# First chunk's q kept in fp32: its bias from one-column products without weight loads in chunk 1, its phi in chunk 3

## The chip, the cores and the metric

The kernel runs on one core of a Trainium2 chip. The metric is the device time of one execution in microseconds. Five engines work side by side, each on its own list of instructions in order, and they wait for each other by semaphores: PE (TensorE, matrix products, into the eight banks of PSUM; its weight loads are listed as PEld), ACT (ScalarE), DVE (VectorE), POOL (GpSimd) and SP (SyncE, which here only sends DMA transfers, in its own order). In the profile a "q" behind a name (SPq) is that engine's instruction queue.

## What is computed

One block with adaptive layernorm: linear attention, then a gated feed-forward part, on 2048 tokens of width 1024. The change lies in the attention's front: layernorm, scale and shift by columns of c's modulation, and the q and k projections with their phi.

```python
mod = (_silu(c) @ w_mod).reshape(c.shape[0], 6, 1, -1)      # sa, ca, ga, sb, cb, gb
h = _layernorm(x, axis=-1) * (1 + ca) + sa
qkv = (h @ wqkv) ...                                        # 32 heads of 32
phi = lambda t: jnp.where(t > 0, t + 1, jnp.exp(t)) + 1e-06
pq, pk = (phi(q), phi(k))
kv = jnp.einsum('bhsd,bhse->bhde', pk, v)
z = jnp.einsum('bhsd->bhd', pk)
o = jnp.einsum('bhqd,bhde->bhqe', pq, kv) / (jnp.einsum('bhqd,bhd->bhq', pq, z)[..., None] + 1e-06)
x = x + ga * (o @ wo)
...
x = x + gb * (silu(h2 @ w_gate) * (h2 @ w_up) @ w_down)     # h2: layernorm of x, scale cb, shift sb
```

## The kernel before, in words

The 2048 tokens go in four chunks of 512, a chunk in four tiles of 128 tokens (tiles 4 to 7 are chunk 1, 12 to 15 chunk 3). The width 1024 goes in eight slices of 128, called dt. Every operation is recorded in the order of the program text; each engine gets its own in that order, and the waits are worked out from the overlaps of what is read and written in SBUF, and from the PSUM banks (lines 63 to 94 and 130 to 166). A write waits for the last writer and the readers of every byte that it covers.

Chunk 0 is special. Its normalized x is transposed on PE while the first loads still arrive. h0_first and h0_scale_only (520, 540) put x times (1+ca) into HT[:, 0]; HT[:, 1] holds the raw transposed x of dt 4 to 7. q_part (685) adds products to the q groups, one group (nt) of 128 output columns in one PSUM bank, as the weights' slices arrive. The shift sa comes later: mod_sc (504) makes columns of the modulation with one-column products, fin_sa (515) copies them out, bias_mm (528) multiplies them with wq, also in one-column products, each with a weight load of its own, and bias_fin (534) copies the eight sums to BIASQ. For dt 6 and 7 the shift is applied before the product. Then q_phi (789) takes each bank to phi: phi_evac (654) does exp and relu on ACT, and phi_flush (666), two groups at a time, the clamp of the exp and the sum on DVE. For a k group, relu is left out, and DVE reads the bank itself (scalar_tensor_tensor into PKT), so that the bank is free only then. E1 and RL have four slots.

After chunk 0's q come its eight k groups (704), then for chunks 1 to 3 eight k groups and eight q groups each (837). Work of other kinds is hung behind a group by its number, in the tables qside, kside, s1, s2 and s3. Layernorm of later tiles: statistics on DVE (462) or as two passes with sums on ACT (act_stats, 574, whose elementwise output is thrown away, for tiles below 8 into HT[:, 1, 0:2, :]), the power on POOL, the normalization ln1_xn on DVE (479), a transpose by DMA into HT (th_dma, 489), and the scale and shift in place, th_mod (493), on DVE, for chunks 2 and 3 every second slice on ACT. macc (711) adds up a row of the modulation from eight slices of STG on DVE, macc_split and mod_red finish it. next_bank (692) deals out the PSUM banks: in turn over eight, from the 40th group on over five.

Behind chunk 3 comes the G stage (909 on): 16 groups of k-transposed times normalized x, with the denominators (den, 937), the reciprocals sent to HBM and read back (RB), kvt_mm (962) on WV, then the output projection and the feed-forward part, some 630 us. The change doesn't touch these.

SP's loads, in order: x of chunk 0, w_mod's ca and wq in pieces, wsa's second half, wq 6 and 7, wsa's first half, two tiles of x, wk's first half, two more, wk's second half, x of tiles 8 to 11 (410 to 431).

Of the kernel before, what the change touches and what calls it, by code (L numbers as in the profile page):

```python
# [5 lines left out]
FP32 = mybir.dt.float32  # L6
# [256 lines left out]
def bass_adaLN_cond__linear_attn_block__swiglu_ffn__prompt_kernel(  # L263
# [22 lines left out]
    with ExitStack() as es:  # L286
# [52 lines left out]
        HT = T("ht", 120 * KB, [128, 2, NDT, 512], BF16)  # L339
        WO = T("wo", 120 * KB, [128, NHG, D], BF16)  # L340
# [74 lines left out]
        sa_load(1)  # L415
# [3 lines left out]
        for j in range(2):  # L419
            P.dma("x1_%d" % j, XRES[:, 4 + j, :], xv[:, 4 + j, :])  # L420
        for i in (1, 0):
            P.dma("wk0%d" % i, WQK[:, 4 * i:4 * i + 4, 1024:1536], wqkvv[:, 4 * i:4 * i + 4, 1024:1536])
        for j in range(2, 4):
            P.dma("x1_%d" % j, XRES[:, 4 + j, :], xv[:, 4 + j, :])
# [68 lines left out]
        def th_mod(ch, dt):  # L493
            buf = ch % 2
            if dt % 2 == 0 or ch == 1:
                P.dve("tensor_scalar", out=HT[:, buf, dt, :], in0=HT[:, buf, dt, :], scalar1=MODCOL[:, 0, dt:dt + 1],
                      scalar2=MODCOL[:, 1, dt:dt + 1], op0=ALU.mult, op1=ALU.add)
            else:
                P.act("activation", out=HT[:, buf, dt, :], in_=HT[:, buf, dt, :], func=ACT.Identity,
                      scale=MODCOL[:, 0, dt:dt + 1], bias=MODCOL[:, 1, dt:dt + 1])  # L500
# [23 lines left out]
        def h0_shift(dt):  # L524
            P.dve("tensor_scalar", out=HT[:, 0, dt, :], in0=HT[:, 0, dt, :], scalar1=MODCOL[:, 1, dt:dt + 1],
                  scalar2=None, op0=ALU.add)

        def bias_mm(dts):
            for nt in range(NDT):
                for dt in dts:  # L530
                    P.pe("matmul", out=PS[:, 0, 16 + nt:17 + nt], lhsT=WQK[:, dt, nt * 128:(nt + 1) * 128],
                         rhs=MODTMP[:, dt:dt + 1], start=False, stop=(dt == 3), skip_group_check=True)

        def bias_fin():
            P.dve("tensor_copy", out=BIASQ[:], in_=PS[:, 0, 16:24])
# [17 lines left out]

        def h0_scale(dt):
            P.dve("tensor_scalar", out=HT[:, 0, dt, :], in0=HT[:, 1, dt, :], scalar1=MODCOL[:, 0, dt:dt + 1],
                  scalar2=MODCOL[:, 1, dt:dt + 1], op0=ALU.mult, op1=ALU.add)
# [97 lines left out]
        def phi_evac(bank, dst, bias=0.0):  # L654
            i = phi_ctr[0] % 4
            phi_ctr[0] += 1
            P.act("activation", out=E1[:, i, :], in_=PS[:, bank, :], func=ACT.Exp, bias=bias)
            if not isinstance(dst, tuple):
                P.act("activation", out=RL[:, i, :], in_=PS[:, bank, :], func=ACT.Relu, bias=bias)
            phi_pend.append((i, dst, bank))  # L660
            if len(phi_pend) == 2:
                phi_flush()
# [29 lines left out]
        def next_bank():  # L692
            i = qk_ctr[0]
            qk_ctr[0] += 1
            return (1, 2, 3, 4, 6, 7, 5, 0)[i % 8] if i < 40 else i % 5 + 1

        def q_group(ch, nt):
            buf, bank = ch % 2, next_bank()
            for dt in range(NDT):
                P.pe("matmul", out=PS[:, bank, :], lhsT=WQK[:, dt, nt * 128:(nt + 1) * 128],  # L700
                     rhs=HT[:, buf, dt, :], start=(dt == 0), stop=(dt == NDT - 1))
            phi_evac(bank, PQT[:, nt, ch * 512:(ch + 1) * 512])

        def k_group(ch, nt):
            buf, bank = ch % 2, next_bank()
            for i, dt in enumerate((6, 7, 4, 5, 0, 1, 2, 3) if ch == 0 else range(NDT)):
                P.pe("matmul", out=PS[:, bank, :], lhsT=WQK[:, dt, D + nt * 128:D + (nt + 1) * 128],
                     rhs=HT[:, buf, dt, :], start=(i == 0), stop=(i == 7))
# [36 lines left out]
        def q_phase_chunk0(side):  # L745
# [7 lines left out]
            for nt in range(7):  # L753
# [5 lines left out]
                q_part(nt, qb[nt], (2, 3))  # L759
            act_stats(4)  # L760
            for nt in range(7):
                if nt == 4:
                    mod_sc(WSA, 0, range(6, 8))
                    fin_sa(6, 2)
                    for dt in (6, 7):
                        h0_scale(dt)
                q_part(nt, qb[nt], (4, 5))
            mod_sc(WSA, 0, range(4, 6))
            fin_sa(4, 2, True)
            for nt in range(7):  # L770
                if nt == 2:
                    bias_mm((4, 5))
                q_part(nt, qb[nt], (6,))
            for nt in range(7):
                if nt == 1:
                    mod_sc(WSA, 0, range(4))
                    fin_sa(0, 4, True)
                    ln_ops[1][0]()
                    ln_ops[1][1]()
                if nt == 4:  # L780
                    bias_mm(range(4))
                    bias_fin()
                q_part(nt, qb[nt], (7,))
            ln_ops[1][2]()
            ln1_rstd1(5)
# [3 lines left out]
            q_phi = lambda nt: phi_evac(qb[nt] if nt < 7 else 0, PQT[:, nt, 0:512], bias=BIASQ[:, nt:nt + 1])  # L789
            for i, dt in enumerate((4, 5, 0, 1, 2, 3, 6, 7)):  # L790
                P.pe("matmul", out=PS[:, 0, :], lhsT=WQK[:, dt, 896:1024], rhs=HT[:, 0, dt, :], start=(i == 0),
                     stop=(i == 7))
            for dt in (4, 5):
                h0_shift(dt)
            ln1_xn(5)
            th_dma(5)
            for dt in range(4):
                h0_shift(dt)
            ln1_xn(4)
            th_dma(4)  # L800
            for nt in range(8):
                q_phi(nt)
                for f in side.get(nt, []):
                    f()
# [5 lines left out]
        qside, kside = {}, {}  # L810
        ln_ops = [ln1_stats_ops(4 + jj) for jj in range(4)]

        def ln_x1(jj):
            for f in ln_ops[jj]:
                f()
            ln1_rstd1(4 + jj)
        for f in ln_ops[2]:
            add(qside, 1, f)
        for f in ln_ops[3]:
            add(qside, 1, f)  # L820
        add(qside, 1, lambda: ln1_rstd2(6))
        for jj in range(2, 4):
            add(qside, 3, lambda jj=jj: ln1_xn(4 + jj))
            add(qside, 3, lambda jj=jj: th_dma(4 + jj))
        for dt in range(NDT):
            add(kside, 1, lambda dt=dt: th_mod(1, dt))
        for jj, k in ((0, 3), (1, 4)):
            add(kside, k, lambda jj=jj: act_stats(10 + jj))
        q_phase_chunk0(qside)
# [25 lines left out]
        for i in range(NDT):  # L855
            add(s1, 8 + i, lambda i=i: stg_load(i))
            add(s2, 1 + i, lambda i=i: wv_load(i))
# [13 lines left out]

        ln_half(2, s1, 0, 0, 1)
# [11 lines left out]
        for kt in range(NDT):  # L884
            add(s2, 4 + kt, lambda kt=kt: macc(STG, kt))
        add(s2, 13, macc_split)
        add(s2, 13, lambda: P.dma("stg1", STG[:], wmv[:, :, 4096:5120]))
        for kt in range(NDT):
            add(s3, 4 + kt, lambda kt=kt: macc(STG, kt))
        add(s3, 14, macc_split)  # L890
        add(s1, 7, lambda: P.pool("memset", ap=MROW[:], constant=0.0))
        add(s1, 7, lambda: P.pool("memset", ap=ZHL[:], constant=0.0))
        s3.setdefault(2, []).extend([mod_red, mod_row_a])
# [321 lines left out]
```

## Time and profile before

| | us |
|---|---|
| median of 3 runs (827.87 to 829.02) | 828.6 |
| the profiled execution's own span, first to last instruction | 827.0 |
| first product of q | 12.71 |
| chunk 0's q phi on DVE, first to last | 31.60 to 39.9 |
| first product of the G stage | 127.27 |
| DMA at 20 to 30 us | 361 GB/s |

| operation (mean time of one) | ns |
|---|---|
| product 128x512 on PE / its weight load | 379 / 98 |
| one-column product | 163 |
| ACT exp or relu from PSUM, no bias / bias from a tile | 604, 600 / 704, 710 |
| DVE read of a k bank (scalar_tensor_tensor) | 682 |
| DVE clamp / sum of a q group | 283 / 414 |
| DVE macc, 128x1024 fp32 | 1279 |
| DVE bn_stats, 512 wide | 675 |

How to read it: an instruction's time holds its latency too, so that products and small instructions overlap; where a cost matters, the distance from start to start is used. A product's end is modelled. In a line of the order of time, "x55" means that 55 of one form came in a row, and a few per cent of matmul records can be missing. "[1.54 <-DMA ht<-xres]" is idle time before the instruction, and what ended it. The granted PE clock is full all through.

### The profile page before, as it was taken

Reading aid. Unit: us, or ns where it says so; the run is one execution under the profiler, and the core shown is the slowest. Engines: PE = TensorE matmul, PEld = TensorE weight load, DVE = VectorE, ACT = ScalarE, POOL = GpSimd, SP = SyncE. Lnnn points to the kernel's source line nnn. Section 1 sums busy time; section 2 is a strip of 40 time slices with the busy share of each in tenths; the row PEclk is TensorE's granted clock in tenths of the full one; section 3 lists DMA queues with packets and bytes.
Section 4 is the critical chain, followed back from the end, with each engine's and each line's share of the span. In section 5 each row is a group of like instructions: output and inputs, shape, how many; then the busy total and the mean of one; then the engine's idle time right before and its main releaser. Section 6 shows DMA issues by size and latency. Waiting matters only on the chain.

```text
span 827.0 us, 10428 instructions
## 1 busy us (share of the span) xinstructions
PE 817.0 (99%) x4244; PEld 376.1 (45%) x4323; DVE 310.8 (38%) x664; ACT 197.3 (24%) x336; POOL 40.7 (5%) x59
## 2 busy tenths in 40 slices
PE   8999999999999999999999999999999999999998
PEld 4544444444444444444444444444444444444444
DVE  5798988476945521111221112122111211221111
ACT  4658643123241111011111101111110111111011
POOL 1010000000130000030000003000000300000000
PEclk9999999999999999999999999999999999999999
DMA  9969665856697995700455570045557004553000
GB/s 317 283 151 225 156 169 144 185 166 200 164 256 234 289 256 153 175 27 23 133 149 152 154 177 29 20 128 153 152 153 185 26 19 124 153 153 87 0 26 26
DMA packets 199360, 119.32 MB, mean 144 GB/s; under 512 B 57992, under 2 KB 183056, under 8 KB 199312
## 3 DMA queue, kind: packets, MB, share of 16 engines
q1 hardware_dynamic: 199296, 118.65, 53.7%
q8 instruction: 34, 0.56, 0.3%
q14 instruction: 14, 0.11, 0.0%
q10 hardware_dynamic: 16, 0.00, 0.0%
HBM read 100.67 MB, written 4.33 MB: 127 GB/s over the span
## 4 chain that ended last, share of the span: by engine, by line
PE 95%; DMA 2%; DVE 1%; SPq 1%; issue 1%; ACT 0%; DVEq 0%; ACTq 0%
PE ps L176 95%; DMA wsa<-in_w_mod_dram 2%; DVE acc L176 1%; SPq L176 1%; DVE pkt L176 0%; DVE e L176 0%; DVE pqt L176 0%; ACT e L176 0%; DVE xres L176 0%; DVE ht L176 0%; DVEq L247 0%; ACTq L247 0%
## 5 line engine op out<-in xcount | busy, mean ns | idle before, releaser
L176 PE MATMUL ps<-h2t,gug 128*128 128x512 bf16 x878 | 210.1, 379 | 0.9
L176 PE MATMUL ps<-h2t,guu 128*128 128x512 bf16 x878 | 209.9, 379 | 0.9
L176 DVE TENSOR_TENSOR at<-sg,ps 128x512 bf16<-128x512 bf16 x112 | 77.0, 688 | 282.7 <-PE ps L176 270.5
L176 ACT ACTIVATE sg<-ps 128x512 bf16<-128x512 f32 x112 | 66.9, 597 | 309.7 <-PE ps L176 298.3
L176 PEld LDWEIGHTS ps<-h2t,guu 128*128 128x128 bf16 x896 | 87.7, 98 | 105.7
L176 PEld LDWEIGHTS ps<-h2t,gug 128*128 128x128 bf16 x896 | 87.6, 98 | 105.5
L176 PE MATMUL ps<-wd_a,at 128*128 128x512 bf16 (+1 forms) x502 | 111.9, 377 | 0.5
L176 PE MATMUL ps<-ht,wqk 128*128 128x512 bf16 x499 | 110.5, 379 | 1.0 <-issue 0.2
L176 PE MATMUL ps<-wd_b,at 128*128 128x512 bf16 (+1 forms) x377 | 84.7, 377 | 0.4
L176 PEld LDWEIGHTS ps<-wd_a,at 128*128 128x128 bf16 x512 | 50.1, 98 | 59.7
L176 DVE TENSOR_TENSOR ut<-att,gb_b 128x512 bf16<-128x512 bf16 (+1 forms) x32 | 13.9, 435 | 167.2 <-ACT att L176 167.2
L176 PEld LDWEIGHTS ps<-ht,wqk 128*128 128x128 bf16 x512 | 49.4, 98 | 59.0 <-DVE ht L176 0.7
L176 ACT ACTIVATE att<-ps 128x512 bf16<-128x512 f32 (+1 forms) x32 | 17.4, 591 | 182.1 <-PE ps L176 182.1
L176 PEld LDWEIGHTS ps<-wd_b,at 128*128 128x128 bf16 x384 | 37.5, 98 | 44.7
L176 PE MATMUL ps<-pk,xres 128*128 128x512 bf16 x250 | 55.4, 379 | 0.6 <-issue 0.5
L176 PE MATMUL ps<-mw,pqt 128*128 128x512 bf16 x249 | 55.5, 379 | 0.5 <-issue 0.2
L176 POOL TENSOR_SCALAR h2t<-h2t,modcol 128x512 bf16<-128x512 bf16 x32 | 26.3, 837 | 383.4 <-DMA h2t<-xn 383.4
L176 ACT ACTIVATE e<-ps 128x512 bf16<-128x512 f32 x56 | 33.2, 604 | 31.9 <-PE ps L176 20.2
L176 PEld LDWEIGHTS ps<-mw,pqt 128*128 128x128 bf16 x256 | 24.7, 98 | 30.2 <-issue 0.5
L176 PEld LDWEIGHTS ps<-pk,xres 128*128 128x128 bf16 x256 | 24.7, 98 | 29.9 <-issue 0.9
L176 ACT ACTIVATE junk<-xres 128x1024 bf16<-128x1024 bf16 x24 | 25.4, 1058 | 34.5 <-DVE xres L176 34.2
L176 DVE SCALAR_TENSOR_TENSOR xres<-ps,xres 128x512 bf16<-128x512 f32 x32 | 21.4, 688 | 11.8 <-PE ps L176 11.6
(107 smaller groups left out, 337.9 us busy)
## 6 DMA issues: line engine op xcount, KB each, us to landing
gug<-in_B_w_gate_dram SPq DMA_DIRECT2D x56, 512.0 KB, 4.0
guu<-in_B_w_up_dram SPq DMA_DIRECT2D x56, 512.0 KB, 5.3
xres<-in_A_x_dram SPq DMA_DIRECT2D x20, 256.0 KB, 4.4
rb<-recip_den SPq DMA_DIRECT2D x8, 512.0 KB, 11.5
stgx<-in_w_mod_dram SPq DMA_DIRECT2D x2, 2048.0 KB, 9.7
wd_a<-in_B_w_down_dram SPq DMA_DIRECT2D x4, 1024.0 KB, 7.4
out_dram<-xres SPq DMA_DIRECT2D x31, 128.0 KB, 1.7
xres<-in_A_x_dram SPq DMA_DIRECT2D x3, 1024.0 KB, 7.1
```

Of the source, the lines that this page charges most:

```text
L176: return getattr(e, method)(**kw)
```

## The change

- The loads: wsa's second half goes behind wq 6, wq 7 and wsa's first half; wk's first half before all four tiles of x.
- Chunk 0's q: no shift is mixed in. Each bank is copied by ACT in fp32 to QPRE (16 KB per partition, where WV will lie); WV's load moves from chunk 2 to the end of chunk 3. The shifted h for k goes to a tile of its own, HS.
- The bias: BIASQ's products move into chunk 1's q groups. Behind each wide product stands one with a single column that uses the weights just loaded. They add up in bank 0, and bias_fin is behind chunk 2's first k group.
- Chunk 0's phi is taken from QPRE in chunk 3, behind groups 1, 3, 4, 6, 9, 11, 13 and 14.
- Chunk 1's layernorm: tiles 5 and 7 on DVE, 4 and 6 on ACT; tile 6's statistics behind the first k group, the rest of it behind the second; th_mod of chunk 1 behind the fifth, every second slice on ACT.
- act_stats of tiles 10 and 11, the stg loads, both rows of macc, macc_split and the first mod_red are hung on other groups.
- The banks: a table for the first 32 groups keeps bank 0 out of chunk 1.

```diff
+        QPRE = T("qpre", 104 * KB, [128, NHG, 512], FP32)
+        HS = T("hs", 144 * KB, [128, NDT, 512], BF16)
...
-        sa_load(1)
         wq_load(6)
         wq_load(7)
         sa_load(0)
...
+        sa_load(1)
+        for i in range(2):
             P.dma("wk0%d" % i, WQK[:, 4 * i:4 * i + 4, 1024:1536], wqkvv[:, 4 * i:4 * i + 4, 1024:1536])
-        for j in range(2, 4):
+        for j in range(4):
             P.dma("x1_%d" % j, XRES[:, 4 + j, :], xv[:, 4 + j, :])
...
-            if dt % 2 == 0 or ch == 1:
+            if dt % 2 == 0:
...
         def h0_shift(dt):
...
+            if dt < 4:
+                P.dve("tensor_scalar", out=HS[:, dt, :], in0=HT[:, 0, dt, :], scalar1=MODCOL[:, 1, dt:dt + 1],
+                      scalar2=None, op0=ALU.add)
+            else:
+                P.dve("tensor_scalar", out=HS[:, dt, :], in0=HT[:, 1, dt, :], scalar1=MODCOL[:, 0, dt:dt + 1],
+                      scalar2=MODCOL[:, 1, dt:dt + 1], op0=ALU.mult, op1=ALU.add)
+
+        def bias_mm(nt, dt):
+            w, v, o = WQK[:, dt, nt * 128:(nt + 1) * 128], MODTMP[:, dt:dt + 1], PS[:, 0, nt:nt + 1]
+
+            def fn(e):
+                return e.add_instruction(mybir.InstMatmult(
+                    start_tensor_calc=(nt == 0 and dt == 0), stop_tensor_calc=(dt == NDT - 1), tile_size=(128, 128),
+                    tile_position=(0, 0), ldweights=False, bass_skip_group_check=True,
+                    name=nc.get_next_instruction_name(), ins=[e.lower_ap(v), e.lower_ap(w)], outs=[e.lower_ap(o)]))
+
+            P.add("pe", fn, reads=[w, v], writes=[o], tag="matmul")
...
+            if i < 8:
+                return (2, 3, 4, 6, 7, 5, 0, 3)[i]
+            if i < 24:
+                return (1, 2, 3, 4, 6, 7, 5)[(i - 8) % 7]
+            if i < 32:
+                return (3, 4, 6, 7, 1, 2, 5, 0)[i - 24]
             return (1, 2, 3, 4, 6, 7, 5, 0)[i % 8] if i < 40 else i % 5 + 1
...
+                if ch == 1:
+                    bias_mm(nt, dt)
             phi_evac(bank, PQT[:, nt, ch * 512:(ch + 1) * 512])
...
+        def q_copy(nt, bank):
+            P.act("activation", out=QPRE[:, nt, :], in_=PS[:, bank, :], func=ACT.Copy)
...
+            for nt in range(7):
+                q_part(nt, qb[nt], (4, 5))
+            for dt in (6, 7):
+                h0_scale_only(dt)
+            for nt in range(7):
+                q_part(nt, qb[nt], (6,))
+            mod_sc(WSA, 0, range(4))
+            fin_sa(0, 4, True)
+            for dt in range(4):
+                h0_shift(dt)
+            for nt in range(7):
+                q_part(nt, qb[nt], (7,))
+                q_copy(nt, qb[nt])
+            q_part(7, qb[0], range(NDT))
+            q_copy(7, qb[0])
+            mod_sc(WSA, 0, range(4, 8))
+            fin_sa(4, 4, True)
+            for dt in range(4, 8):
+                h0_shift(dt)
             act_stats(4)
...
+            for j in (5, 7):
+                for f in ln_ops[j - 4]:
+                    f()
+                ln1_rstd1(j)
+            ln1_xn(5)
+            th_dma(5)
             for f in act_mv_ops(4):
                 f()
             neg_rstd(4)
...
+            ln1_xn(7)
+            th_dma(7)
             ln1_xn(4)
             th_dma(4)
...
+        add(kside, 0, lambda: act_stats(6))
+        for f in act_mv_ops(6):
+            add(kside, 1, f)
+        add(kside, 1, lambda: neg_rstd(6))
+        add(kside, 1, lambda: ln1_xn(6))
+        add(kside, 1, lambda: th_dma(6))
         for dt in range(NDT):
-            add(kside, 1, lambda dt=dt: th_mod(1, dt))
-        for jj, k in ((0, 3), (1, 4)):
+            add(kside, 4, lambda dt=dt: th_mod(1, dt))
+        for jj, k in ((0, 6), (1, 7)):
             add(kside, k, lambda jj=jj: act_stats(10 + jj))
...
-            add(s1, 8 + i, lambda i=i: stg_load(i))
-            add(s2, 1 + i, lambda i=i: wv_load(i))
+            add(s1, 4 + i, lambda i=i: stg_load(i))
+            add(s3, 15, lambda i=i: wv_load(i))
...
+        add(s2, 0, bias_fin)
+        for nt, k in enumerate((1, 3, 4, 6, 9, 11, 13, 14)):
+            add(s3, k, lambda nt=nt: phi_evac(None, PQT[:, nt, 0:512], bias=BIASQ[:, nt:nt + 1],
+                                                       src=QPRE[:, nt, :]))
...
-            add(s2, 4 + kt, lambda kt=kt: macc(STG, kt))
-        add(s2, 13, macc_split)
...
+            add(s1 if kt < 4 else s2, (12, 13, 14, 15, 0, 1, 2, 3)[kt], lambda kt=kt: macc(STG, kt))
+        add(s2, 4, macc_split)
...
-            add(s3, 4 + kt, lambda kt=kt: macc(STG, kt))
-        add(s3, 14, macc_split)
+            add(s2 if kt < 6 else s3, (10, 11, 12, 13, 14, 15, 0, 1)[kt], lambda kt=kt: macc(STG, kt))
+        add(s3, 3, macc_split)
```

## The prediction

> **What bounds the kernel now.** I read the page's busy line first, then the busy time by 10 us stages, then PE, ACT, DVE and SP in order of time around the change.
>
> ```profile
> span 827.0 us, 10428 instructions
> PE 817.0 (99%) x4244; PEld 376.1 (45%) x4323; DVE 310.8 (38%) x664; ACT 197.3 (24%) x336; POOL 40.7 (5%) x59
> ```
>
> PE is full, so little can be won elsewhere. The stages (PE, PEld, DVE, ACT, POOL busy us with counts, clock, DMA share, GB/s) show how near the helpers are:
>
> ```profile
> 30.00:40.00 10.00, 9.95 (x47) 4.58 (x47) 9.90 (x32) 9.11 (x17) 0.92 (x2) 1.00 1.14 247
> 40.00:50.00 10.00, 9.95 (x47) 4.38 (x47) 8.46 (x31) 8.67 (x16) 0.00 (x0) 1.00 0.76 160
> 60.00:70.00 10.00, 9.95 (x47) 4.47 (x46) 8.51 (x27) 9.52 (x18) 0.80 (x1) 1.00 1.11 180
> 90.00:100.00 10.00, 9.95 (x47) 4.51 (x46) 9.97 (x22) 8.08 (x16) 0.00 (x0) 1.00 0.46 107
> ```
>
> DVE and ACT, 38% and 24% busy over the span, are nearly full here: PE stays fed only because eight PSUM banks let DVE run late. In order of time on PE (start, length):
>
> ```profile
> 16.81 0.94 PE L176 MATMUL ps<-siluc,wca 128*128 128x1 bf16 x32
> 27.24 0.94 PE L176 MATMUL ps<-modtmp,wqk 128*128 128x1 bf16 x32
> 28.04 12.25 PE L176 MATMUL ps<-ht,wqk 128*128 128x512 bf16 x55
> 127.27 3.62 PE L176 MATMUL ps<-pk,xres 128*128 128x512 bf16 x15
> ```
>
> 32 one-column products with their weight loads last 0.80 us (27.24 to 28.04), 25.3 ns each. At 28.04 chunk 0 lacks 11 of its 64 wide products; with the other groups that is 459 up to 127.27: 99.2/459 = 0.216 us each, 1.728 per group of eight. From 28.04 on PE hardly waits. Chunk 0's k begins at 28.04 + 11x0.216 = 30.42, chunk 1 at 44.24.
>
> ```profile
> 37.36 2.61 SPq L176 DMA_TRANSPOSE ht<-xres  x2
> 40.02 2.40 SPq L176 DMA_DIRECT2D xres<-in_A_x_dram  x4
> 43.10 2.67 DVE L176 TENSOR_SCALAR ht<-ht,modcol 128x512 bf16<-128x512 bf16 x8 [1.54 <-DMA ht<-xres]
> 63.10 1.06 ACT L176 ACTIVATE junk<-xres 128x1024 bf16<-128x1024 bf16 x1
> 64.16 0.58 ACT L176 ACTIVATE e<-ps 128x512 bf16<-128x512 f32 x1
> ```
>
> Chunk 1's h was just in time: its transposes landed at 43.1, the eight scalings ended at 45.77, and PE began chunk 1 at 44.24.
>
> **The front of chunk 0: a gain.** The 48 bias products go: 48 x 25.3 ns = 1.21 us. Between 17.62 (end of the products of w_mod's ca part, 16.81 + 32x0.0253) and 28.04 PE did 33 wide (7.13) and 112 one-column products (2.83); the other 0.46 us were waits for wsa and MODTMP, which now have later uses. DMA order: landing goes by bytes, and 8.36 MB had moved when wsa's second half landed at 25.7, about 1 MB more than was queued up to it. By that rule the half now needed first, with 6.3 MB queued up to it, lands near 22.8 (7.02 MB had moved at 22, 7.75 at 24), and PE gets there at 17.62 + 29x0.216 = 23.9; the second lands at 25.7, needed at 27.9; wk's last megabyte is unmoved at 34.4, needed at 35.9. All are covered, by 1 to 2 us. K starts at 30.42 - 1.21 - 0.46 = 28.74. Its products 5 to 8 wait for four shifts (DVE is free 0.52 after the last small product, 26.59 to 27.11, then 0.28 each): 0.25 us. **Net -1.42.** The eight copies take ACT 0.5 to 0.66 each (PSUM copies into mw, fp32 writes into gtmp) and end near 29; the first reaches its bank 0.4 us before q's last group needs it.
>
> **The statistics of tile 6: the main term.** The change puts act_stats(6) on ACT behind the first k group. For tiles below 8 its throw-away output goes to HT[:, 1, 0:2], where the transposes of tiles 5, 7 and 4 have just been sent. The program's dependency tracking makes ACT wait until all three have landed (and what they wrote there is overwritten). Queued behind it on ACT are the exps of k groups 1 to 7, and behind these DVE's flushes, which free PSUM. Step by step:
>
> - DVE is free at 28.74 + 0.52 + 4x0.28 = 30.4. Two tiles' statistics at 1.6 each (27.11 to 28.74): 33.6; xn of 5 and 7 and tile 4's small operations (0.5, 0.35, 0.5), POOL's power, xn of 4: 35.9.
> - SP issues the transposes 1.3 apart (four in 5.37 at 56.71): 34.2, 35.5, 36.85. Landing: 3.3 unhindered, 7.7 for the first of this chunk, 4.4 for its last (38.65 to 43.1), which also had four x loads sent behind it. I take 4.4: **41.2** (40.2 to 44.5).
> - ACT: two passes 2.25 (61.92 to 64.16), 43.55; exp of K1 0.6; DVE's clamp 0.2 and two PSUM reads at 0.61: 45.6. K7 shares bank 3 with K1 in the new table; it was due at 28.99 + 7x1.728 = 41.08 and starts at 45.7: **+4.6**.
> - Tile 6's small operations, power and xn 1.8: 47.4. Its transpose, now behind the four x loads on SP (sent by 41, so long gone), lands 3.3 later, 50.8. th_mod now alternates DVE and ACT: ACT's four at 0.71 end at 53.75, so chunk 1's first group ends at 54.1; K7 ended at 47.43, so it should have at 49.16: **+4.9**.
> - Behind th_mod on ACT: exps of K5 and K6 (0.96), act_stats(10) 2.25, exp of K7 0.6, then DVE 1.42: K7's bank 3 is free at 59.0. Chunk 1's third group wants it at 55.8: **+3.2**.
>
> Before, that group began at 47.70: 11.3 later in all.
>
> **One-column products in chunk 1: a cost.** 64 of them, no loads of their own. No row shows a second product on loaded weights. Below: 9.8 ns (128 products of 32 columns in 1.26 us at 167.41), 0.63 us. Above: the next load, now behind the small product, is laid open at its full 98 ns: 6.3. I take the like row, load and product for 25.3 ns: **+1.6**. The Trainium skill, "TensorE: Matmul & The Clock Gate", section "The mechanism", speaks against the change: a weight load overlaps running products only where its row group differs, and here all use every row. By that rule each next load would lie open, and this term would be an estimated 64 x 98 ns = 6.3 us. The rows differ from it: loads of 98 ns at the same rows vanish in a 0.216 us pace, and pairs run at 25.3.
>
> **DVE's new load: a second stall.** Four macc (0.67 + 3x1.2) move from chunk 2 into chunk 1's q half, and four more plus the split (1.86, 99.16 to 101.02) into chunk 2's k half, where DVE used to catch up. ACT rules chunk 1's q half: Q0 closes at 59.0 + 7x1.728 + 0.2 = 71.3, then seven more exp-relu pairs at 0.96, two act_stats at 2.25, four th_mod at 0.71: Q7 is ready at 86.5, the pair before at 84.6. From there DVE: that pair 0.9, four xn 1.9, two macc 2.4, last pair 1.1, macc 1.2, copy 0.15, macc 1.2, two k pairs 3.2, three macc 3.6, split 1.9, half a k pair 1.0: 103.2. The table gives K4 of chunk 2 and its first q group the same bank 1, four groups apart instead of eight. That q group is due at 59.0 + 14x1.728 + 1.6 + 8x1.728 = 98.6: **+4.6** (0 to 7). If the one-column products cost more, this wait shrinks by as much, since its end doesn't depend on them.
>
> **Covered.** The stg loads move four groups ahead, into time in which SP has only pk's transposes to send, and macc wants them four groups after. Chunk 3's eight exp-relu pairs and DVE's 0.57 each: ACT has 1.7 us per group and needs 1.0 + 1.2 at most; by the same sums k banks come free 0.5 us early, at worst a stall of 1. The weights WV are sent at the end of chunk 3, 34 us before kvt needs them; but 2 MB (5.8 us at 361 GB/s) stand ahead of the z row and recip_den. The slack there is 0.9 us (G's seventh evacuation ends at 166.5, kvt starts at 167.41), and the loads should be mostly gone: 0, at most +5.
>
> **Sum.** -1.42 + 4.6 + 4.9 + 3.2 + 1.6 + 4.6 = +17.5 on the span of 827.0: 844.5. The median before (828.6) is 1.6 above the span: **846**.
>
> **Rivals.**
> - *One stall only*: DVE keeps up in chunk 2. For it: before, DVE caught up there by 83. Against: 7 us more work. 846 - 4.6 = 841.4. Chance 0.2.
> - *The transposes land before ACT gets there*, so act_stats(6) costs only itself. Then tile 6's transpose goes out behind four x loads near 40.6 and lands near 44; ACT's scalings hold chunk 1's first group to 47.3 and its third to 52.2 (+4.5): with the products 834.7, with the second stall 839.3. Against: they are sent 2 to 4 us after ACT is ready. Chance 0.09.
> - *Everything is covered* (the other side): PE keeps only its own change, -1.42 + 0.63 to 1.6: 827.8 to 828.8, no change. Its mechanism is PSUM slack; it decides only if the last of the three transposes lands by 36.7 (K7's due time less the 4.4 from landing to a free bank), and by my sum it isn't even issued then. Even with free products it would be 827.2. Chance 0.07.
> - *The products aren't what the change says* (they take weight loads after all): 25.3 ns each, the price taken; no other time.
> - *More*: kvt or open weight loads on top, 851 and over. Chance 0.06.
>
> **How the numbers follow.** Forecast 0.58, its own range 841 to 850. The range runs from 836, leaving out only the covered case and part of the second, to 851 (the late landing or WV on top). Within 0.2% (1.7 us, about what a measurement can tell) is most of the covered case, 0.05; its rest, 0.02, goes to faster, which needs free products and another gain that I don't see; slower 0.93.
>
> **What would show it.** PE idle near 41 to 46, 47 to 54 and 56 to 59, and before chunk 2's q; ACT's junk pass near 41 waiting for DMA ht; exps of K1 to K7 bunched after 43; one-column products at about 25 ns; chunk 0's k starting near 28.7. I am wrong if ACT's junk pass starts by 37, if PE shows no gap there, or if the G stage grows.

## The result, and the profile after

| | median us (all runs) | against the kernel before |
|---|---|---|
| before | 828.39 (827.87 to 829.02) | |
| after | 847.78 (847.26 to 850.41) | 1.0239 [1.0227, 1.0252], slower |
| predicted | 846.0 (836 to 851) | |

The change costs 19.4 us. The profiled execution of after has a span of 848.4 us; it is the longest of five, whose other spans are 845.2 to 846.4. First the page's span and busy lines:

```profile
span 848.4 us, 10404 instructions
PE 825.4 (97%) x4260; PEld 375.6 (44%) x4275; DVE 311.1 (37%) x661; ACT 206.0 (24%) x352; POOL 41.8 (5%) x60
```

DVE is as busy as before (311.1 against 310.8 us), and ACT has 8.7 us more. The span grew by 21.4, and PE's busy time by 8.4 alone: most of the loss is idle PE. The order of time on PE (start, length, idle time ahead and its releaser) shows where:

```profile
28.73 0.81 PE L176 MATMUL ps<-hs,wqk 128*128 128x512 bf16 x3
...
44.86 3.39 PE L176 MATMUL ps<-hs,wqk 128*128 128x512 bf16 x8 [3.43 <-DVE mv L176]
50.01 5.78 PE L176 MATMUL ps<-ht,wqk 128*128 128x512 bf16 x16 [1.76 <-DVE ht L176]
57.73 12.44 PE L176 MATMUL ps<-ht,wqk 128*128 128x512 bf16 x48 [1.94 <-DVE pkt L176]
103.61 39.25 PE L176 MATMUL ps<-ht,wqk 128*128 128x512 bf16 x165 [4.43 <-DVE pkt L176]
147.94 3.62 PE L176 MATMUL ps<-pk,xres 128*128 128x512 bf16 x16
```

Chunk 0's k begins at 28.73. Its last group K7 waits 3.43 us, chunk 1's first group 1.76, its third group 1.94, chunk 2's first q group 4.43. The G stage begins at 147.94 instead of 127.27: of the 21.4 us, 20.7 are there by then. Its length to the first long run of the output projection is unchanged: 65.16 us, against 65.17 before (127.27 to 192.44). The last 0.7 is one short wait in the output projection.

ACT and SP in the same view, around the first of these waits:

```profile
34.42 4.09 SPq L176 DMA_TRANSPOSE ht<-xres  x3
38.56 2.02 SPq L176 DMA_DIRECT2D xres<-in_A_x_dram  x4
40.44 1.06 ACT L176 ACTIVATE ht<-xres 128x1024 bf16<-128x1024 bf16 x1 [8.63 <-DMA ht<-xres]
42.68 2.14 ACT L176 ACTIVATE e<-ps 128x512 bf16<-128x512 f32 x4
```

ACT stands still for 8.63 us in front of tile 6's first pass, until the three transposes have landed. The two passes then write over what has just landed, slices 0 and 1 of tiles 5, 7 and 4, so chunk 1's h is wrong there in after: the wait is the sign of a fault in the order, which every run below that leaves the passes in place shares. Behind the two passes four exps come in one block at 42.68; they had been ready, one after the other, since about 32. DVE can read K1's bank only then (43.50 to 44.8, with its neighbour's), and K7 wants that bank. (The releaser named for K7, DVE mv, is the small operation that begins when this read ends, at 44.72.)

One thing is there that I had not foreseen. Busy time by stages on PE (length, PE busy with the count of products that touch the stage, granted clock, DMA share, GB/s):

```profile
45.00:46.00 1.00, 1.00 (x3) 0.50 0.00 0
104.00:106.00 2.00, 2.00 (x6) 0.50 1.14 210
106.00:108.00 2.00, 2.00 (x6) 0.50 0.86 205
108.00:110.00 2.00, 2.00 (x8) 0.66 1.05 398
110.00:112.00 2.00, 2.00 (x11) 1.00 1.02 349
```

With each wait the granted clock goes to 0.50 for a while, and PE, though fully busy, makes about half the products: 6 touch two microseconds at 0.50, 11 once the clock is full. Before showed 1.00 all through. In stretches of a quarter of a microsecond the low clock lasts 3.42 us with each of the first three waits (44.5 to 47.9, 51.3 to 54.7, 58.1 to 61.6) and 6.83, twice as long, with the fourth (102.5 to 109.4).

### The profile page after: what moved, and what is told of

It reads as the page before. It is cut to its first block, busy times and chain, and to the rows that moved or that the text cites. A ratio compares the mean times of both kernels' runs of the same rounds, so it can differ in the third digit from the quotient of the medians.

```text
span 848.4 us, 10404 instructions
## 1 busy us (share of the span) xinstructions
PE 825.4 (97%) x4260; PEld 375.6 (44%) x4275; DVE 311.1 (37%) x661; ACT 206.0 (24%) x352; POOL 41.8 (5%) x60
## 4 chain that ended last, share of the span: by engine, by line
PE 89%; DVE 4%; ACT 2%; DMA 2%; issue 1%; POOL 0%; SPq 0%; ACTq 0%; DVEq 0%
PE ps L176 89%; DVE acc L176 1%; ACT ht L176 1%; DMA ht<-xres 1%; DMA mhlt<-mhl 1%; DVE pkt L176 1%; ACT e L176 1%; DVE xres L176 0%; DMA xres<-in_A_x_dram 0%; DVE mhl L176 0%; ACT junk L176 0%; DVE stats L176 0%; DVE e L176 0%; DVE red L176 0%; ACT rl L176 0%
## 5 line engine op out<-in xcount | busy, mean ns | idle before, releaser
L176 PE MATMUL ps<-ht,wqk 128*128 128x512 bf16 x436 | 104.6, 396 | 9.0 <-DVE pkt L176 6.4
L176 PEld LDWEIGHTS ps<-ht,wqk 128*128 128x128 bf16 x448 | 44.3, 101 | 68.5 <-DVE pkt L176 7.4
L176 ACT ACTIVATE junk<-xres 128x1024 bf16<-128x1024 bf16 x24 | 25.3, 1056 | 35.2 <-DVE xres L176 34.9
L176 DVE TENSOR_SCALAR e<-e 128x512 bf16<-128x512 bf16 x64 | 17.1, 288 | 25.2 <-ACT e L176 24.7
## 6 DMA issues: line engine op xcount, KB each, us to landing
rb<-recip_den SPq DMA_DIRECT2D x8, 512.0 KB, 11.4
```

The costliest lines, as they stand in the source:

```text
L176: return getattr(e, method)(**kw)
```

## The experiments

The theory was the prediction's own: the loss consists of waits, made by where work was put (tile 6's statistics behind transposes in flight; banks that return after four groups), and the work added to PE is small. The rivals were that the moved work itself fills DVE and ACT, so that a wait taken away comes back elsewhere, and that the one-column products open their weight loads.

**Tile 6's junk to another place.** Tile 6's passes no longer write where the transposes land, which also mends the fault; nothing moves.

```diff
-            junk0 = HT[:, 1, 0:2, :] if st < 8 else JUNK1
+            junk0 = HT[:, 1, 0:2, :] if st < 6 else JUNK1
```

> The changed kernel, but tile 6's two statistics passes on ACT throw their output into a tile of its own instead of HT[:, 1, 0:2], so that they wait for no transposes. Theory (the wait for the transposes starts the chain of stalls): the passes start near 31.8 instead of 40.4, k group 7 of chunk 0 starts without a gap at 41.1, chunk 1's first group ends at 47.3 to 48.3 and its third starts at 52.3 to 53.3 instead of 57.7; later stages as before; time 842 to 844, that is 4 to 6 us less. Rival (ACT and DVE simply have too much to do there, the wait is only where it shows): less than 1 us.

Measured: 843.18 us, 1.0178 [1.0163, 1.0193]. PE in order of time:

```profile
45.69 5.35 PE L176 MATMUL ps<-ht,wqk 128*128 128x512 bf16 x16 [2.44 <-DVE ht L176]
53.39 10.75 PE L176 MATMUL ps<-ht,wqk 128*128 128x512 bf16 x49 [2.35 <-DVE pkt L176]
97.59 37.84 PE L176 MATMUL ps<-ht,wqk 128*128 128x512 bf16 x168 [4.42 <-DVE pkt L176]
```

K7's wait is gone: chunk 0's k runs without a wait for a bank from 28.83 to 43.25. The waits behind it stay, because tile 6's transpose and ACT's four scalings still come late, and chunk 2's wait is as long as it was (4.42), only six microseconds earlier. A wait set by the order of DVE's work moves along with the work ahead of it.

**A ring of eight banks through chunk 2.** K4 of chunk 2 and its first q group no longer share a bank.

```diff
-            if i < 32:
-                return (3, 4, 6, 7, 1, 2, 5, 0)[i - 24]
-            return (1, 2, 3, 4, 6, 7, 5, 0)[i % 8] if i < 40 else i % 5 + 1
+            if i < 40:
+                return (3, 4, 6, 7, 1, 2, 5, 0)[i % 8]
+            if i < 48:
+                return (4, 5, 1, 2, 3, 6, 7, 0)[i - 40]
+            return i % 5 + 1
```

> The changed kernel, but from chunk 2 on the PSUM banks come round only after eight groups (six to eight across the change of chunks), instead of four for chunk 2's k groups 4 and 5. Theory A (the bank table makes chunk 2's first q group wait): no gap at 99, G stage 7.3 us earlier (4.5 of waiting and 2.8 of half clock after it), time 840 to 841. Theory B (DVE has too much work, the table only says where it shows): the wait comes back in chunk 3, less than 3 us gained.

Measured: 844.12 us, 1.0185 [1.0168, 1.0202]; 3.7 less than after, about half of what was expected. The wait in front of chunk 2's q is gone, and a new one stands in front of chunk 3. PE and DVE in order of time:

```profile
113.50 0.75 DVE L176 TENSOR_SCALAR acc<-stg,siluf 128x1024 f32<-128x1024 bf16 x1 [3.10 <-DMA stg<-in_w_mod_dram]
116.90 21.32 PE L176 MATMUL ps<-ht,wqk 128*128 128x512 bf16 x98 [2.44 <-DVE ht L176]
```

DVE waits 3.10 us for the second load of the modulation weights, and chunk 3's last scaling stands behind the multiply-adds that follow. In after the 4.43 us ahead had hidden this. So the wait was real, and a part of what it cost comes back.

**Both edits together.**

> The two single edits together: tile 6's and 7's junk goes to the other space, and the banks go round eight apart from chunk 1's second half on. Theory A (the two losses are separate waits): the gains add, 847.8 - 4.6 - 3.7 = 839.5, so 839 to 840.5. Theory B (the second wait is set by DVE work that starts at a fixed time, so that what is won before it is lost there): 841.5 to 843.

Measured: 841.27 us (839.94 to 841.80), 1.0155 [1.0139, 1.0171]: 6.5 us less than after, where the single edits give 4.6 and 3.7. The median lies between the two expectations, and the run doesn't decide between them. Its trace has the same new wait in front of chunk 3 (2.54), here, in the profiled execution, with the slow clock behind it: the 98 products take 23.01 us, where they took 21.32 with the longer ring alone. These 1.7 us are about what is missing from the sum.

**Nineteen extra products into the gap ahead of chunk 2's q part**, to keep PE's clock up while it waits.

```diff
+            if ch == 2 and nt == 0:
+                for _ in range(19):
+                    P.pe("matmul", out=PS[:, 7, :], lhsT=WQK[:, 0, 0:128], rhs=HT[:, 0, 0, :], start=True, stop=True)
```

> The changed kernel, with 19 more wide products into a free bank ahead of chunk 2's first q group, in the 4.4 us in which PE waits there; their results are overwritten. Theory (an idle PE is granted only half its clock for some us afterwards): the clock stays full at 103 to 110, the first 13 products behind the gap take 0.216 instead of 0.427, 2.8 us less: 844.5 to 845.5. Rival (the slow products have another cause, such as transfers at that time): no gain, or a loss.

Measured: 846.74 us (846.06 to 847.66), 1.0219 [1.0204, 1.0234]. PE by stages, where after's rows above had 0.50 and 0.66:

```profile
104.00:106.00 2.00, 2.00 (x11) 1.00 0.98 186
106.00:108.00 2.00, 2.00 (x11) 1.00 1.04 386
```

Full clock, 11 products in 2 us instead of 6: the slow clock is a result of the gap, and not of what runs behind it. The median gains 1.0 us, less than the 2.3 to 3.3 expected, and the ranges of the two kernels overlap. The expectation was taken from after's profiled execution, its slowest, and how long the clock stays low differs: behind the same gap (4.43 and 4.42 us) it is 6.83 us in after and 3.42 in the run with the junk moved, where the same stretch of 168 products takes 37.84 us instead of 39.25. Chance shows earlier in this trace too, where nothing was changed. PE in order of time:

```profile
45.23 1.90 PE L176 MATMUL ps<-hs,wqk 128*128 128x512 bf16 x8 [3.43 <-DVE mv L176]
50.38 5.25 PE L176 MATMUL ps<-ht,wqk 128*128 128x512 bf16 x16 [3.25 <-DVE ht L176]
```

Behind the same 3.43 us as in after, K7 runs at full clock here (1.90 us instead of 3.39). Nothing is won by it: the next wait grows from 1.76 to 3.25, and chunk 1 begins 5.15 us behind K7 in both.

**The one-column products, the loads the other way round.** The product with one column goes first and loads the weights, the wide one uses them.

```diff
-                P.pe("matmul", out=PS[:, bank, :], lhsT=..., rhs=HT[:, buf, dt, :], ...)
-                if ch == 1:
-                    bias_mm(nt, dt)
+                if ch == 1:
+                    P.pe("matmul", out=PS[:, 0, nt:nt + 1], lhsT=..., rhs=MODTMP[:, dt:dt + 1], ...)
+                    wide_mm(bank, buf, nt, dt)
```

> The changed kernel, with each pair in chunk 1's q groups turned round: the one-column product comes first with the weight load, the wide one second without. If the 25.3 ns per pair come from the next weight load that the one-column product lays open, the pace of a pair falls from 0.241 to near 0.22; if a product has a shortest slot of its own whatever its width, it stays at 0.241. The time should stay within 1 us of the changed kernel's either way, because chunk 2's first q group waits for DVE and not for PE.

Measured: 847.99 us in one run. PE in order of time, two small products that follow each other, with a wide one between them that is left out here; first this kernel, then after:

```profile
72.01 0.16 PE L176 MATMUL ps<-modtmp,wqk 128*128 128x1 bf16 x1
72.25 0.17 PE L176 MATMUL ps<-modtmp,wqk 128*128 128x1 bf16 x1
```

```profile
70.00 0.17 PE L536 MATMUL ps<-modtmp,wqk 128*128 128x1 bf16 x1
70.25 0.17 PE L536 MATMUL ps<-modtmp,wqk 128*128 128x1 bf16 x1
```

From one to the next it is 0.24 us in either order: 0.216 for the wide product and 25 ns for the small one, whoever loads. The expectation's 0.22, for a next load laid open by the small product, is out.

**Only 8 of the 64 one-column products.** The other 56 are left out, so that chunk 1's part computes an incomplete bias.

```diff
-                    start_tensor_calc=(nt == 0 and dt == 0), stop_tensor_calc=(dt == NDT - 1), ...
+                    start_tensor_calc=(nt == 0 and dt == 0), stop_tensor_calc=True, ...
...
-                if ch == 1:
+                if ch == 1 and dt == 0:
```

> As after, but of the 64 one-column products in chunk 1's q part only the 8 with the first slice of the inputs are issued, so that 56 are left out and chunk 1's q bias is incomplete. Theory A (a product costs its 25 ns on PE alone): the stretch of chunk 1's first q groups shrinks by 56 x 0.0253 = 1.4 us, and the time by 0 to 1.4, less where the end of the stretch is set by the wait in front of chunk 2: 846.4 to 847.8. Theory B (each product also opens a weight load of about 98 ns): 56 x 0.098 = 5.5 us, 842.3.

Measured: 848.49 us (847.00 to 849.24), 1.0240 [1.0221, 1.0258]: no gain, 0.7 above the first bracket, and far from the 842.3 of open weight loads. In order of time:

```profile
69.34 1.89 PE L176 MATMUL ps<-ht,wqk 128*128 128x512 bf16 x8
71.09 1.89 PE L176 MATMUL ps<-ht,wqk 128*128 128x512 bf16 x8
102.78 39.39 PE L176 MATMUL ps<-ht,wqk 128*128 128x512 bf16 x168 [5.69 <-DVE pkt L176]
```

A group with one small product takes 1.75 us, 8 x 0.216 + 0.025. The stretch gets shorter, and the wait in front of chunk 2's q grows. The fair comparison is the run before this one, which like it has no slow clock behind chunk 1's third group: 5.69 us instead of 4.46, nearly the 1.4 that PE saved, and the wait ends 44.1 us behind the start of that third group instead of 44.2. Its end doesn't depend on the products, as the prediction had it. PE's weight loads number 4275 with 8 small products, as with 64: they take none.

**Tile 6 earlier, the banks far apart, ACT with two of chunk 1's scalings instead of four.** This undoes the order, and with it the fault, and keeps the rest of the change: bias, fp32 copies and the late phi. Tile 6's passes stand straight behind tile 4's, its normalization and transpose straight behind tile 4's transpose.

```diff
+            act_stats(6)
...
+            for f in act_mv_ops(6):
+                f()
+            neg_rstd(6)
...
+            ln1_xn(6)
+            th_dma(6)
...
-            if dt % 2 == 0:
+            if (dt % 2 == 0 and ch != 1) or (ch == 1 and dt not in (2, 5)):
...
-                return (1, 2, 3, 4, 6, 7, 5)[(i - 8) % 7]
+                return (1, 2, 4, 6, 7, 5, 3)[(i - 8) % 7]
+            if i < 40:
+                return (4, 6, 7, 5, 3, 1, 2, 0)[i % 8]
+            if i < 48:
+                return (4, 5, 1, 2, 3, 6, 7, 0)[i - 40]
```

> What it changes against after: tile 6's sum of squares comes straight behind tile 4's on ACT, so ahead of the transposes that land in its junk space, and its normalization and transpose go behind tile 4's in the same stage; of chunk 1's eight modulations ACT does two instead of four; the banks go round seven and eight groups apart up to the end of chunk 3. Theory A (the loss over before is made of waits in three places, 3.4 in front of K7, 4 to 5 in front of chunk 1's first group and between its groups, 4.4 with a slow stretch of PE behind it in front of chunk 2's q part, and the work that was added to PE is small): the waits close but for one of about 2 to 4 us in front of chunk 3, whose modulation comes behind a wait of DVE for the second load of the modulation weights as in the run with the longer ring (2.44 there), so 832 to 835. Theory B (the moved copies and shifts cost DVE and ACT what the waits seem to cost, so a wait removed opens another one as large): 840 or more.

Measured: 833.59 us (832.03 to 834.54), 1.0065 [1.0047, 1.0083]: 14.2 of the 19.4 us are back, as the first theory had it. One wait is left before the G stage, which begins at 131.55. Three things were changed at once here, so the run doesn't say what each is worth. In order of time on PE:

```profile
28.49 14.42 PE L176 MATMUL ps<-hs,wqk 128*128 128x512 bf16 x64
42.74 14.19 PE L176 MATMUL ps<-ht,wqk 128*128 128x512 bf16 x65
103.46 23.01 PE L176 MATMUL ps<-ht,wqk 128*128 128x512 bf16 x98 [2.40 <-DVE ht L176]
```

**The multiply-adds spread, the shifts of chunk 0 earlier**, on top of this, against the wait in front of chunk 3. The first two lines of each sign in the diff are the first row of the modulation, the last two the second; the third moves the second load of the modulation weights (stg1). The shifts go ahead of chunk 0's last q group.

```diff
-            add(s1 if kt < 4 else s2, (12, 13, 14, 15, 0, 1, 2, 3)[kt], ...)
-        add(s2, 4, macc_split)
-        add(s2, 5, ... "stg1" ...)
+            add(s1 if kt < 2 else s2, (14, 15, 1, 3, 4, 5, 7, 8)[kt], ...)
+        add(s2, 9, macc_split)
+        add(s2, 9, ... "stg1" ...)
...
-            add(s2 if kt < 6 else s3, (10, 11, 12, 13, 14, 15, 0, 1)[kt], ...)
-        add(s3, 3, macc_split)
+            add(s2 if kt < 2 else s3, (14, 15, 1, 2, 5, 8, 10, 12)[kt], ...)
+        add(s3, 14, macc_split)
```

> As b1_early, and the sixteen multiply-adds of chunk 1's to chunk 3's vector work are spread so that the second load of the modulation weights starts later and nothing stands behind it; the shifts of the second half of chunk 0 come ahead of the last first-half q group, so that no matmul waits 0.25 us for them. Theory A: no wait over 1 us is left from chunk 0's K part to the end of chunk 3; what PE has more than before is 48 + 64 one-column products of 25.3 ns (2.8 us) with a front that begins 1.2 to 1.7 earlier, so 829 to 831. Theory B: DVE is late somewhere in chunk 2 or 3 by more than it was in before: 834 to 838.

Measured: 837.12 us, 1.0102 [1.0086, 1.0118]: 3.5 worse than without the spread. The number lies in the second theory's bracket, but not for its reason: PE waits for DVE nowhere in chunks 2 and 3. PE and SP in order of time:

```profile
127.28 3.62 PE L176 MATMUL ps<-pk,xres 128*128 128x512 bf16 x16
134.46 4.61 SPq L176 DMA_DIRECT2D wv<-in_A_wqkv_dram  x8
139.12 0.50 SPq L176 DMA_DIRECT2D z_row<-zr  x1
150.48 6.78 PE L176 MATMUL ps<-pk,xres 128*128 128x512 bf16 x24 [3.71 <-DVE g L176]
```

Up to the G stage there is no wait left, and it begins at 127.28, against 127.27 before. But my spread put the second split's transpose in front of the loads of WV, and these stand on SP ahead of the write of the normalizer row; its reload is sent 9.5 us later than in before (144.09 instead of 134.56), and the first evacuations of G wait for it.

**WV in the G stage**, in two forms: the first with the spread as it was, the second with its end three groups earlier.

```diff
-            add(s3, 15, lambda i=i: wv_load(i))
...
+            if g == 2:
+                for i in range(NDT):
+                    wv_load(i)
```

> As b2_spread, but the eight loads of the value weights are issued in the G stage behind the third group, instead of at the end of chunk 3, where they held SP for 4.6 us (134.46 to 139.07) ahead of the write and the reload of the normalizer row, which the first G evacuation waits for. Theory A (b2's loss behind the G stage's start, which had stood at 127.28 against 127.27 in before, is this queue): the reload is issued some 4 us earlier, the wait of 3.71 us in the G stage goes, 828.5 to 830. Theory B (the multiply-adds that I placed late in chunk 3 hold DVE, and so the G evacuations, back): most of b2's loss stays, 833 to 836.

> As b4_wv, with the second round of multiply-adds ended by chunk 3's tenth group and the split and its transpose behind the twelfth, instead of the thirteenth and fifteenth. Theory A: no gain over b4_wv, 828.5 to 830, within 0.3% of before: the 112 one-column products (2.8 us) weigh what the earlier front gives. Theory B: 1 to 3 us less than b4_wv, and 828.5 to 830.5.

Measured: 842.47 us, 1.0171 [1.0157, 1.0185], and 842.64 us, 1.0175 [1.0161, 1.0189]. Both miss: the wait for g is gone, and a longer one for WV itself takes its place, in the first form 6.72 us and then 0.4 to 0.5 in front of each further slice (7.48 first in the second form). The loads are sent at 155.43, behind the reloads of the reciprocals. The two forms agree within 0.2 us, so where the multiply-adds end doesn't matter here. In order of time, first form:

```profile
173.50 0.22 PE L176 MATMUL ps<-g,wv 128*32 128x32 bf16 x4 [6.72 <-DMA wv<-in_A_wqkv_dram]
```

**WV at the end of chunk 3, the split well ahead of it.**

```diff
-            add(s2 if kt < 2 else s3, (14, 15, 1, 2, 5, 8, 10, 12)[kt], ...)
-        add(s3, 14, macc_split)
+            add(s2 if kt < 2 else s3, (14, 15, 0, 1, 2, 3, 4, 5)[kt], ...)
+        add(s3, 7, macc_split)
```

> As b2_spread with the value weights loaded at the end of chunk 3 again, and the second round of multiply-adds ended by chunk 3's sixth group, so that the split and its transpose stand some 9 us ahead of those loads, as in b1_early (transpose at 119.2, loads at 130.6), and not just in front of them (132.8 and 134.5 in b2_spread). Theory A (every wait that the change brought is a matter of order, and what stays is 112 products of 25.3 ns against an earlier front): the G stage begins at 127.3 as in b2_spread, has no wait, and the time is 828.5 to 829.5, within 0.2% of before. Theory B (the loads in the G stage's front cost something in any order): 831 or more.

Measured: 835.91 us, 1.0089 [1.0075, 1.0103]: the first theory misses by 6.4 us, and the second, that these loads cost something in any order, is not refuted by it. DVE is now late in chunk 3 (a wait of 1.42 us in front of the group there, G stage from 128.65), the loads of WV go out at 133.55, 4.9 us behind the G stage's start, where in the run without the spread they went out 0.9 ahead of it, and the G stage up to kvt took 40.1 us as in before. The reload of the row follows at 142.40, and G's evacuations are late again (1.01 and 2.04 us on PE).

**WV between the reload of the row and the output weights, the scaling of the queries later.**

```diff
                 z_row()
+                for i in range(NDT):
+                    wv_load(i)
...
-            if 6 <= g <= 9:
-                fold_ga(2 * (g - 6))
-                fold_ga(2 * (g - 6) + 1)
+            if 7 <= g <= 10:
+                fold_ga(2 * (g - 7))
+                fold_ga(2 * (g - 7) + 1)
...
-            if 7 <= g < 15:
-                scale_pq(g - 7)
+            if 11 <= g < 15:
+                scale_pq(2 * (g - 11))
+                scale_pq(2 * (g - 11) + 1)
```

(The load of the next modulation weights, which reuses the first half of RB, goes from the eleventh to the thirteenth group.)

> As b4_wv (G stage begins at 126.57 in its profile, 0.7 earlier than in before), with the value weights loaded in the G stage behind the reload of the normalizer row and ahead of the output weights, and the queries scaled behind the eleventh G group instead of the seventh, so that DVE doesn't hold a G evacuation back for the reloaded reciprocals, which the 2 MB of value weights delay; the fold of the gate goes one group later. Theory A (all that is left is order): no wait over 1 us in the G stage, so before's time less 0.7, 827.5 to 829. Theory B (before's G stage had no room for 2 MB of loads, and any place costs the transfer): 5 us or more behind before's 828.4, 833 or more.

Measured: 830.31 us (829.78 to 830.90, 11 runs), 1.0017 [1.0008, 1.0026]. The bracket of the first theory is missed by 1.3 us, the second is out by 2.7. In order of time on PE:

```profile
127.56 3.62 PE L176 MATMUL ps<-pk,xres 128*128 128x512 bf16 x16
...
167.70 1.26 PE L176 MATMUL ps<-g,wv 128*32 128x32 bf16 x128
...
177.32 0.43 PE L176 MATMUL ps<-wo,kvt 32*32 32x512 bf16 x13 [0.55 <-DVE g L176]
```

The G stage keeps one wait of 0.55, and kvt starts at 167.70, against 167.41 in before. In the profiled spans (829.1 us against 827.0), 0.3 of the 2.1 us are there when the G stage begins, 0.9 more behind the wait for g, and 0.8 more behind one of 0.71 in the output projection. So 17.5 of the 19.4 us were a matter of order, banks and the split between ACT and DVE, and not of the work added: 2 MB of loads do fit into the G stage, once what waits for the transfers behind them is moved too. No version here beats the kernel before.

## Why the prediction was right, and where it was off

| step | predicted | after's trace |
|---|---|---|
| chunk 0's k begins; wait for the shifts | 28.74; 0.25 | 28.73; 0.26 |
| transposes of 5, 7, 4 landed, ACT's pass starts | 41.2 | 40.44 |
| K7 starts | 45.7 | 44.86 |
| chunk 1's third group starts | 59.0 | 57.73 |
| one-column products, each | 25.3 ns | 25 ns |
| chunk 2's first q group: due, starts | 98.6, 103.2 | 99.0, 103.6 |
| G stage grows by | 0 (at most 5) | 0 |
| G stage begins later by | 17.5 | 20.67 |

- **The front** was right to 0.01 us, which is partly chance: in other runs with the same front k begins anywhere from 28.5 to 29.8.
- **Tile 6's statistics** as the main term: shown for the first wait. The three waits are where they were said to be. With the junk moved, the first goes, chunk 1's third group starts 4.3 us earlier, and the time falls by 4.6. The second and third go in the run that moves tile 6 ahead, but there the banks and the split of the scalings changed with it, and their shares are not shown apart. The step was sized 1.3 us too large (the third group starts 10.0 later than in before, not 11.3), most of it from the transposes: they landed 3.0 to 3.4 us behind their issue, and not the 4.4 that I had taken from a transpose with loads behind it.
- **The products** at 25 ns: shown by the pace of the pairs in both orders and by the group with one of them; the count of weight loads, 4275 against 4323 before, falls by just the 48 of the old bias products, so the rival that they load after all is out. The Trainium skill, "TensorE: Matmul & The Clock Gate", section "The mechanism", says that a load overlaps running products only at another row group; the pace of 0.24 us with loads of 98 ns at the same rows contradicts that sentence. The section also lets a load into a background weight buffer go ahead, which would fit these rows; the prediction left that out. The same page, section "Wait — 56ns, not 53.3ns?", gives products a least distance of about 25 ns however few their columns are, and the 25 ns agree with that. For the products that the profile lists as 128*32 it doesn't hold: kvt's 128 pass in 1.26 us.
- **That the products and the wait in front of chunk 2 trade one for one** was said, and is shown by the run with 8 of them: 1.23 us more wait than with 64 at the same clock, no gain in time.
- **The second stall**: from due to start 4.6 for 4.6 (4.43 of it idle), from the shared bank, and it goes with the longer ring. From chunk 1's third group to chunk 2's first q the prediction has 44.2 us; the three runs that stop at this bank without a slow clock on the way show 44.1 to 44.2, after, with it, 45.9. So that the start itself was met (103.2 for 103.6) is luck: 1.3 too late and 1.7 of clock left out. That half its gain comes back in front of chunk 3 was not in the prediction, nor needed for it.
- **WV at no cost**: right for after, whose split stands early enough. It is cover and not slack: with another order in front of it on SP, the same loads held the normalizer row back, and the kernel was 8.8 us behind before; sent too late, they held kvt back, and it was 14.0 behind.
- **What the sum lacked is a term**: the slow clock behind the waits. I carried the pace of 0.216 us over from a trace that never stops. In after's profiled execution 49 products (the line shows 48, one record is missing) from 57.73 on take 12.44 us instead of 49 x 0.216 + 0.16 = 10.7, and 168 from 103.61 on take 39.25 instead of 36.45: 1.7 and 2.8 us. The low clock behind the first two waits costs nothing, because what releases the next group, ACT and DVE, is late anyway; the run with nineteen extra products shows it for K7. Then 10.0 + 1.7 + 1.6 + 4.6 + 2.8 = 20.7, the measured 20.67. The span's miss is thus 3.9 us (848.4 for 844.5: 4.5 of clock and 0.7 in the output projection, less the 1.3). In the median it is 1.8 (847.8 for 846.0): the profiled execution had the lowest mean clock of five, 0.990, the others 0.992 to 0.996. So the mechanism was right, but that the number came this close owes something to luck: two sizes were off in opposite directions.

Of the rivals, "one stall only" and "everything is covered" fell with the four waits; "the transposes land before ACT gets there" fell with ACT's 8.63 us. "More", with kvt late or loads laid open, didn't come: the G stage kept its length.

## What to carry to other kernels

Where eight banks let a helper engine run late, look at what an instruction overwrites, even with output that is thrown away: a pass put behind transfers in flight stops its engine's whole queue, and the loss appears on PE groups later, at a bank. Ask also whether what it overwrites is still needed; here it was. Undoing one wait of such a chain pays only up to the next one; here it took the order of ACT, DVE, the banks, SP and two moved consumers together to get 17.5 of 19.4 us back. When a sum opens gaps on PE, add a term for the clock behind them: here 1.7 us (half of 3.42) and once 2.8 for gaps of 2 to 4.5 us, sometimes nothing, and only where PE itself sets what comes next.

## What was not expected of the hardware

- The granted clock fell to 0.50 with waits of 1.76 to 5.69 us and stayed there for 3.42 us or twice that, 6.83, in every trace in which PE had work throughout behind the wait. It fell 2.3 to 4.9 us after PE went idle, behind the shorter waits when PE was already running again: after's second wait ended at 50.01, and the clock fell at 51.3. Other waits of like length cost nothing of the kind, such as 2.35 us with the junk moved and 2.44 with the longer ring; 3.43 us in front of K7 lowered the clock in after and didn't in the run with nineteen extra products.
- Within a trace the changes of the clock lie whole multiples of 3.41 us apart (in after 44.49, 47.91, 51.32, 54.73, 58.15, 61.56, 102.52 and 109.35), wherever the waits are. Between two such ticks, PE's busy share tells what comes at the second. From 36 to 190 us of the twelve traces with a fall, the clock fell at the end of every stretch in which PE was busy for 43% or less and of none with 54% or more; from 44 to 53% it did either. A low clock rose behind every stretch that was busy for 84% or more, and behind none with 76% or less.
- With that the cases above come out. The 3.43 us in front of K7 lie in one stretch in after (10% busy) and are split by a tick in the run with the extra products (51 and 48%). PE works for 68% of the first slow stretch in front of chunk 2's q in after, so a second one follows; with the junk moved it is 84%, and none does.
- These bounds were read off traces made for other ends; no run set the share on purpose, and what decides between 44 and 53% stays open.
- The Trainium skill, "TensorE: Matmul & The Clock Gate", section "What's actually happening", names a free-running window of about 3.4 us, an idle one lowering the clock and a busy one raising it. The 3.42 and 6.83 us agree with that, as one and two windows, and the ticks show that it runs free of the kernel. That a wait of 1.76 us was enough is less than the whole idle window that it asks for: a stretch that was busy for 45% lowered the clock.
- The reload of the reciprocals to all partitions is slow: each of its eight transfers of 512 KB takes 11.4 to 11.6 us from issue to landing (medians of before, after and the runs with WV moved), and DVE stood 8.2 us in front of it in the run with WV behind it on SP (6.0 in before, where PE didn't wait for it).
